# Block 0 takes all sixteen weight pieces in one run, decays are relative to the end of a 128-token block, and the start has another written order

## The chip, the cores and the metric

The kernel runs on one core of one Trainium2 chip. The time is in device microseconds (us), the median of several runs of the whole program. TensorE is called PE, its weight loads PEld, VectorE DVE, ScalarE ACT, GpSimd POOL, SyncE SP. SP and POOL issue the DMAs that are spoken of here.

## The reference

A gated linear attention over 768 tokens, 4 batches and 8 heads of 48 channels, whose output is the input of a feed-forward layer with a squared ReLU:

```python
f = 1.0 / (1.0 + np.exp(-f_logit))
for t in range(S):
    state = f[:, :, t, :, None] * state + np.einsum('bhd,bhe->bhde', k[:, :, t], v[:, :, t])
    y[:, :, t] = np.einsum('bhd,bhde->bhe', q[:, :, t], state)
...
x = attn_out.transpose(0, 2, 1, 3).reshape(B * S, H * D)
h = x @ w_in            # (3072, 384) @ (384, 2048)
r = np.maximum(h, 0.0)
return (r * r) @ w_out  # (2048, 384)
```

## The kernel before, in words

The 768 tokens are cut into six blocks of 128. A block has 4 x 128 = 512 tokens over the batches, the columns of nearly every large operation. The feed-forward layer cuts its 2048 hidden channels into 16 pieces f. For each piece `up` multiplies x by w_in (9 matmuls of 512 columns: three parts of the 384 channels, and three products of high and low halves each), `square` (ACT, three operations) and `rest` (DVE) make the high and low halves of the squared result, and `down`, two pieces later, adds 9 matmuls of w_out into three PSUM banks. Two PSUM banks take turns for `up`, so `up` of a piece waits for `rest` of the piece two before it.

Weights arrive as raw words, 32 loads of 384 KB (piece f, i = 0 for w_in and 1 for w_out), and are decoded once: two operations on ACT, two on DVE each. A decoded piece lies where its raw words lay.

Attention works in 24 units: unit n is head pair n % 4 of block n // 4. A unit of the first three pairs loads f, k, q (`fkq`, 768 KB) and v (`vn`). `gates` (ACT) makes sigmoids. `keys` (DVE) scans them backwards for the decay from each token to the end of its chunk, POOL limits the chunk's whole decay `pe` from below, and the keys are multiplied. `queries` inverts `pe`, scans forwards and multiplies the queries. PE turns the keys (`turn`; ACT copies them out), later blocks do it by DVE and DMA. PE makes the products for the state (`add`) and the scores, DVE masks the scores, `states` carries the state from chunk to chunk, PE makes the output `py`, and ACT and DVE split it into the halves of x (`upper`, `lower`). The fourth pair takes its inputs from rows that `move` has copied by DMA from the other three. Its output `ys` is copied by DMA into spare rows of the three parts of x (`parts`), six copies a block. Pieces 0 and 1 of block 0 don't need these copies: they multiply `ys` itself with a fourth part of w_in (`up_fourth`, raw words `raw4`).

A chunk has 64 tokens before, two to a block. So a unit has 8 chunks, `pe` 8 columns, and `states` decays and adds twice (in block 0, where there is no state yet, once less).

The order of the start is written by hand: FIRST and SECOND are lists of steps, a letter for the step and the number of the unit or piece, recorded in this order on every engine. f, p, z, L, v are loads, G gates, K keys, Q queries, T and N the turn and its copy, D add, S scores, M mask, C states, r and s copies for the crossed halves, Y outputs, H and X the split, m the moves, g and h the copies into x, i and o loads of weights, A I c J and B O d P their four decoding steps, u and U `up`, R `square`, E `rest`, W `down`. Each engine runs its instructions in the recorded order. `busy` steps are matmuls on ones, whose result isn't used.

Before, SECOND ends with block 0's first eight pieces (0 to 7). Then block 1 runs with all sixteen, decoding pieces 8 to 15 on the way (`hook`, with a small memset `mark` ahead of each such load), then block 0 again with pieces 8 to 15, then blocks 2 to 5. `keep` copies block 0's first half out of PSUM into `part`, and `finish` adds it to the second half. The attention units 8 to 23 stand at SLOTS, counted in pieces behind the end of SECOND.

Of the kernel before, what the change touches and what calls it, by code (L numbers as in the profile page):

```python
# [12 lines left out]
F32 = mybir.dt.float32  # L13
# [6 lines left out]
AF = mybir.ActivationFunctionType  # L20
# [12 lines left out]
NZ = B * NC  # L33
CZ = C + 1
# [12 lines left out]
AHEAD = 4  # L47
LO = 8
# [16 lines left out]
SLOTS = (12, 14, 19, 21, 22, 28, 31, 34, 37, 44, 47, 50, 53, 60, 63, 66, 69)  # L65
# [5 lines left out]
f0 G0 p0 K0 f1 G1 z0 p1 T0 N0 v0 D0 Q0 r0 K1 T1 f2 G2 p2 z1 N1 C0 S0 v1 D1 i0 A0 Q1 m1 M0 v2 K2 z2 Q2 S1  # L71
r1 C1 L4 busy3 T2 j0 s0 i2 Y0 N2 I0 S2 D2 m0 H0 M1 X0 s1 Y1 e0 G4 n0 v3 D3 c0 K4 a0 J0 M2 m2 busy2 S3 T4
C2 H1 X1 r2 o0 B0 O0 i1 A1 s2 busy3 Y2 o1 I1 v4 A2 c1 H2 r3 d0 C3 I2 c2 s3 B1 v6 ua0 J1 L5 G5 M3
"""
SECOND = """
ua1 X2 ub1 i3 P0 A3 ub0 Q4 w0 J2 Y3 H3 N4 uc0 X3 uc1 r4 g3 O1 U0 d1 K5 i4 o5 S4 D4 T5 R0 I3 E0 c3 U1 i5
W0 v5 A5 C4 M4 J3 A4 I4 I5 s4 Y4 o4 R1 H4 E1 h3 U3 P1 U2 o2 B2 Q5 N5 X4 O2 L6 c4 v7 i7 i6 G6 K6 S5 c5 W1
M5 J4 o3 R3 E3 B4 O4 m5 T6 D5 C5 R2 B3 J5 B5 E2 U4 d2 O3 r5 P2 s5 Y5 O5 A6 U5 A7 N6 d3 P3 I6 H5 X5 o6 W2
R4 d4 Q6 o7 P4 E4 B7 D6 S6 d5 P5 W3 M6 C6 W4 c6 J6 r6 s6 m4 R5 I7 B6 O6 c7 Y6 H6 d6 J7 U6 O7 d7 X6 P6 m6
E5 r7 D7 R6 S7 C7 M7 U7 E6 s7 Y7 H7 X7 R7 h7 W5 W6 g7 P7 E7  # L80
# [3 lines left out]
class Moe:  # L84
# [40 lines left out]
    def decode(self, row, parts):  # L125
# [5 lines left out]
        head = self.head[self.heads % HEADS][:rows, :n]  # L131
# [7 lines left out]
        )  # L139
        yield  # L140
# [177 lines left out]
    def keep(self, po):  # L318

        part = self.third_of("part0")  # L320
        for e in range(NJ):
            (self.nc.vector.tensor_copy if e % 2 else self.nc.scalar.copy)(out=part[e], in_=po[e])
        return part

# [30 lines left out]
def chunks(t):  # L355
    return t.rearrange("p (n t) -> p n t", t=C)
# [6 lines left out]
def fast_path(ctx, tc, moe, ident, low, fkqT, vN, w, w4, out):  # L363
# [28 lines left out]
    V.memset(dr[:, C::CZ], 1.0)  # L392
# [15 lines left out]
    class Unit:  # L408
# [36 lines left out]
        def gates(self):  # L445
            nc.scalar.activation(scanned(self.fz[:, 1:])[:, :, :C], chunks(self.ft), AF.Sigmoid)  # L446
# [626 lines left out]
```

## Time and profile before

| | us |
|---|---|
| median of 3 runs | 489.99 (489.88 to 490.95) |
| span of the profiled execution | 489.3 |
| PE busy | 471.9 (96%) |
| ACT busy | 284.3 (58%) |
| DVE busy | 248.9 (51%) |
| PEld busy | 377.5 (77%) |
| POOL busy | 29.7 (6%) |

The span runs from the first to the last instruction. The profile lists no time of its own for the profiled execution beside it; the runs shown are 0.6 to 1.7 us above the span. Busy times are unions over an engine's instructions. PE's include the latency of pipelined matmuls, so a busy PE need not be at its peak; the gaps that the timeline shows on it are the surer reading. A timeline row gives the start, the length, the engine, the line, the operation, what it writes and reads, how many instructions are merged in it, and in brackets the idle time of the engine before it and what ended that.

### The profile page before, as it was taken

To read this page: it belongs to the slowest core of one execution; us is meant where nothing else is said; L and a number is where in the kernel's file an instruction comes from. 1 tells how busy PE (TensorE), PEld (TensorE's weight loads), DVE (VectorE), ACT (ScalarE), POOL (GpSimd) and SP (SyncE) were. 2 spreads that over 40 slices of the span, in tenths; PEclk is the share of its full clock that TensorE was granted. 3 is DMA by queue.
4 is the path that set the end of the run, shared out by engine and by line. 5 is a ranking of instruction groups with operands and counts; after the bars stand their busy time and mean duration, and the time that the engine had idled before them with its cause. 6 is when DMAs were issued, how large, how long until landed. Compare 5 with 4: busy or idle time off the path is not lost.

```text
span 489.3 us, 11451 instructions
## 1 busy us (share of the span) xinstructions
PE 471.9 (96%) x4775; PEld 377.5 (77%) x4775; DVE 248.9 (51%) x456; ACT 284.3 (58%) x591; POOL 29.7 (6%) x66
## 2 busy tenths in 40 slices
PE   2889999999999999999999999999999999999996
PEld 2667777888788888888888788888888887888884
DVE  7999962678575365727335636434643322211112
ACT  4589874976755564656565665664745442534441
POOL 4411000000000000000000000000000000000000
PEclk9899999999999999999999999999999999999999
DMA  8888107582544525360423470134440001100002
GB/s 288 246 301 289 31 6 254 162 275 57 108 113 137 122 37 161 80 150 1 105 41 101 118 157 10 37 92 109 122 90 3 1 2 33 68 0 0 1 0 70
DMA packets 64748, 48.65 MB, mean 99 GB/s; under 512 B 46912, under 2 KB 50352, under 8 KB 64688
## 3 DMA queue, kind: packets, MB, share of 16 engines
q1 hardware_dynamic: 64096, 46.78, 34.6%
q0 software_dynamic: 448, 0.92, 0.9%
q8 instruction: 39, 0.64, 0.6%
q14 instruction: 21, 0.17, 0.1%
q10 hardware_dynamic: 144, 0.13, 0.1%
HBM read 35.22 MB, written 7.86 MB: 88 GB/s over the span
## 4 chain that ended last, share of the span: by engine, by line
PE 91%; DMA 5%; DVE 1%; ACT 1%; issue 1%; SPq 1%; POOL 0%; DVEq 0%; ACTq 0%
PE po L276 41%; PE ph L249 41%; DMA raw<-in_w_dram 3%; PE ds L561 2%; PE ds L550 2%; PE py L609 2%; DMA vn<-in_vN_dram 1%; PE ph L621 1%; PE ph L609 1%; PE py L621 1%; SPq L439 1%; DMA x<-ys 1%; DVE fkq L465 0%; ACT rx L487 0%; ACT ys L638 0%
## 5 line engine op out<-in xcount | busy, mean ns | idle before, releaser
L249 PE MATMUL ph<-x,w 128*128 128x512 f32 x864 | 218.2, 398 | 0.8 <-DVE sc L568 0.4
L249 PEld LDWEIGHTS ph<-x,w 128*128 128x128 f32 x864 | 161.6, 188 | 41.3 <-DMA x<-ys 1.2
L276 PE MATMUL po<-gh,w 128*128 128x512 f32 x576 | 180.9, 395 | 0.0
L266 DVE TENSOR_TENSOR gl<-ph,gh 128x512 fp32r<-128x512 f32 x96 | 66.4, 692 | 219.5 <-ACT gh L261 218.3
L259 ACT ACTIVATE ph<-ph 128x512 f32<-128x512 f32 x96 | 56.1, 585 | 147.6 <-PE ph L249 147.6
L276 PEld LDWEIGHTS po<-gh,w 128*128 128x128 f32 x576 | 108.3, 188 | 25.1
L276 PE MATMUL po<-gl,w 128*128 128x512 f32 x288 | 115.9, 402 | 0.0
L276 PEld LDWEIGHTS po<-gl,w 128*128 128x128 f32 x288 | 54.1, 188 | 13.9 <-DVE gl L266 0.7
L261 ACT CAST gh<-ph 128x512 fp32r<-128x512 f32 x96 | 56.4, 587 | 3.0
L260 ACT ACTIVATE ph<-ph 128x512 f32<-128x512 f32 x96 | 55.9, 582 | 3.0
L456 POOL TENSOR_SCALAR fkq<-fkq 128x8 f32<-128x8 f32 x18 | 12.3, 685 | 284.2 <-DVE fkq L451 124.3
L495 ACT COPY sx<-sp 48x208 f32<-48x208 f32 x44 | 16.1, 365 | 16.0 <-DVE sp L583 15.4
L451 DVE TENSOR_TENSOR_SCAN fkq<-fz,dr 128x520 f32<-128x520 f32 x18 | 22.2, 1232 | 2.1 <-ACT fz L446 2.1
L465 DVE TENSOR_TENSOR_SCAN fkq<-fz,dz 128x520 f32<-128x520 f32 x18 | 22.4, 1242 | 0.6
L609 PEld LDWEIGHTS py<-sc,vn 64*48 64x48 f32 (+1 forms) x384 | 16.2, 126 | 7.3 <-issue 7.3
L145 ACT CAST w<-wa 128x384 fp32r<-128x384 f32 (+1 forms) x33 | 16.6, 511 | 7.9 <-DVE wa L136 7.7
L609 PE MATMUL py<-sc,vn 64*48 64x64 f32 (+1 forms) x384 | 20.6, 222 | 0.0
L133 ACT CAST head<-raw 128x384 f16<-128x384 bf16 (+1 forms) x33 | 19.6, 628 | 1.2 <-DMA raw<-in_w_dram 1.1
L621 PE MATMUL py<-rx,sx 48*48 48x64 f32 x192 | 19.3, 215 | 0.0
L147 DVE TENSOR_TENSOR w<-wa,w 128x384 fp32r<-128x384 f32 (+1 forms) x33 | 18.0, 548 | 1.1 <-ACT w L145 0.6
L136 DVE SCALAR_TENSOR_TENSOR wa<-raw,head 128x384 int32<-128x384 int32 (+1 forms) x33 | 17.5, 548 | 1.3 <-ACT head L133 1.3
L159 ACT ACTIVATE junk<-w 128x384 f32<-128x384 f32 x32 | 16.8, 526 | 0.1
(105 smaller groups left out, 443.6 us busy)
## 6 DMA issues: line engine op xcount, KB each, us to landing
raw<-in_w_dram SPq DMA_DIRECT2D x32, 383.8 KB, 5.8
fkq<-in_fkqT_dram SPq DMA_DIRECT2D x15, 768.0 KB, 6.3
vn<-in_vN_dram SPq DMA_DIRECT2D x24, 192.0 KB, 4.0
steps<-fkq SPq DMA_DIRECT2D x48, 64.0 KB, 2.2
out_dram<-ob SPq DMA_DIRECT2D x12, 256.0 KB, 2.1
kn<-steps SPq DMA_DIRECT2D x12, 224.0 KB, 3.2
fkq<-in_fkqT_dram SPq DMA_DIRECT2D x9, 256.0 KB, 5.0
x<-ys SPq DMA_DIRECT2D x30, 64.0 KB, 2.4
```

What stands on the lines that cost most here:

```text
L133: nc.scalar.copy(out=self.upper(head, F16), in_=high)
L147: nc.vector.tensor_tensor(out=w[:, 1], in0=a, in1=w[:, 0].bitcast(F32), op=ALU.subtract)
L249: self.nc.tensor.matmul(self.ph[f], lhsT=w[:, i], rhs=x[:, j], start=first and n == 0, stop=last and n == 2)
L259: nc.scalar.activation(ph, ph, AF.Relu)
L260: nc.scalar.activation(ph, ph, AF.Square)
L261: nc.scalar.copy(out=gh, in_=ph)
L266: self.nc.vector.tensor_tensor(out=gl, in0=self.ph.pop(f), in1=gh.bitcast(F32), op=ALU.subtract)
L276: self.nc.tensor.matmul(po[e], lhsT=l, rhs=r, start=f == fs[0] and i == 0, stop=f == fs[-1] and i == 2,)
L451: V.tensor_tensor_scan(out=rr[:, ::-1], data0=self.fz[:, NZ * CZ : 0 : -1], data1=dr[:, ::-1], initial=0.0, op0=ALU.mult, op1=ALU.add,)
L465: V.tensor_tensor_scan(out=pp, data0=self.fz[:, : NZ * CZ], data1=dz, initial=0.0, op0=ALU.mult, op1=ALU.add)
L609: nc.tensor.matmul(self.py[c][h * C : h * C + m, b * C : (b + 1) * C], lhsT=self.vn[rows, b, h * D : h * D + m], rhs=self.sc[rows, h, b], ...
L621: nc.tensor.matmul(self.py[c][h * C : h * C + m, b * C : (b + 1) * C], lhsT=s[rows, b * D : b * D + m], rhs=q[rows], start=False, stop=b = ...
```

## The change

A chunk of the decays is now the whole block: scans have 4 starts instead of 8, `pe` has 4 columns, and decays are relative to the end of 128 tokens. The state products of both halves of a block then share one reference, so `states` decays once at the start of a block and adds twice. In block 0 nothing is decayed: `first_state` (step k, ACT) copies the first half's products out of PSUM, and `states` adds the second half.

Block 0 takes all sixteen pieces in SECOND, with all 32 weights loaded and decoded there; `keep`, `part`, the second visit to block 0 and the memsets `mark` go. Units 8 and 9 have some of their steps in SECOND (L8, K8, Q8, t8, b8, L9, v8). A unit whose `fkq` buffer comes free late is loaded later (`frees`). FIRST and SECOND are written anew throughout.

```diff
-NZ = B * NC
-CZ = C + 1
+NZ = B
+CZ = TB + 1
-SLOTS = (12, 14, 19, 21, 22, 28, 31, 34, 37, 44, 47, 50, 53, 60, 63, 66, 69)
+SLOTS = (5, 8, 10, 12, 14, 20, 23, 26, 29, 36, 39, 42, 45, 52, 55, 58, 61)
 FIRST = """
-f0 G0 p0 K0 f1 G1 z0 p1 T0 N0 v0 D0 Q0 r0 K1 T1 f2 G2 p2 z1 N1 C0 S0 v1 D1 i0 A0 Q1 m1 M0 v2 K2 z2 Q2 S1
+f0 busy3 f1 p0 G0 z0 p1 v0 f2 G1 K0 T0 v1 N0 j0 D0 i3 K1 z1 Q0 o0 p2 Q1 T1 S0 busy2 m1 z2 G2 M0 i0 r1
...
 def chunks(t):
-    return t.rearrange("p (n t) -> p n t", t=C)
+    return t.rearrange("p (n t) -> p n t", t=TB)
...
+        def first_state(self):
+            nc.scalar.copy(out=self.sp[:, 1, : B * D], in_=self.ds[:ROWS, 0, : B * D])
+
         def states(self):
-            s2 = at = state[self.hp]
-            for c in range(NC):
-                pd = self.ds[:ROWS, c, : B * D]
-                if self.blk == 0 and c == 0:
-                    at = pd
-                    continue
-                sp = self.sp[:, c, : B * D].rearrange("p (b e) -> p b e", e=D)
+            s2 = state[self.hp]
+            sp = [self.sp[:, c, : B * D] for c in range(NC)]
+            if self.blk:
                 V.tensor_tensor(
-                    out=sp, in0=at.rearrange("p (b e) -> p b e", e=D),
-                    in1=self.pe[:ROWS, c::NC].unsqueeze(2).broadcast_to([ROWS, B, D]),
-                    op=ALU.mult,
+                    out=sp[0].rearrange("p (b e) -> p b e", e=D),
+                    in0=s2.rearrange("p (b e) -> p b e", e=D),
+                    in1=self.pe[:ROWS].unsqueeze(2).broadcast_to([ROWS, B, D]), op=ALU.mult,
                 )
+            for c in range(self.blk == 0, NC):
                 V.tensor_tensor(
-                    out=s2.rearrange("p (b e) -> p b e", e=D), in0=sp,
-                    in1=pd.rearrange("p (b e) -> p b e", e=D), op=ALU.add,
+                    out=(*sp, s2)[c + 1], in0=sp[c], in1=self.ds[:ROWS, c, : B * D], op=ALU.add
                 )
-                at = s2
...
-        part = []
-        owed = moe.ending(lambda po: part.extend(moe.keep(po)))
-        whole = half[0] + half[1]
-        order = [(1, whole), (0, half[1])] + [(blk, whole) for blk in range(2, NBLK)]
+        owed = ended(0)
+        order = [(blk, whole) for blk in range(1, NBLK)]
```

What the tables do shows in the order of the instructions. The first place is DVE at the start, from the first scan on; numbers in the names are block and head pair. Before:

```order
L451 SCALAR_TENSOR_TENSOR fkq0_0_141<-fz0_73,dr_69 128x520
L457 TENSOR_TENSOR fkq0_0_141<-fkq0_0_141 128x512
L463 RECIPROCAL dz_70<-fkq0_0_141 128x8
L465 SCALAR_TENSOR_TENSOR fkq0_0_141<-fz0_73,dz_70 128x520
L468 TENSOR_TENSOR fkq0_0_141<-fkq0_0_141 128x512
L451 SCALAR_TENSOR_TENSOR fkq0_1_152<-fz1_74,dr_69 128x520
L457 TENSOR_TENSOR fkq0_1_152<-fkq0_1_152 128x512
L583 TENSOR_TENSOR sp0_75<-ds0_0_167,fkq0_0_141 112x192
L588 TENSOR_TENSOR state0_81<-sp0_75,ds0_0_167 112x192
L463 RECIPROCAL dz_70<-fkq0_1_152 128x8
```

Now:

```order
L444 SCALAR_TENSOR_TENSOR fkq0_0_141<-fz0_73,dr_69 128x516
L450 TENSOR_TENSOR fkq0_0_141<-fkq0_0_141 128x512
L444 SCALAR_TENSOR_TENSOR fkq0_1_147<-fz1_74,dr_69 128x516
L450 TENSOR_TENSOR fkq0_1_147<-fkq0_1_147 128x512
L456 RECIPROCAL dz_70<-fkq0_0_141 128x4
L458 SCALAR_TENSOR_TENSOR fkq0_0_141<-fz0_73,dz_70 128x516
L461 TENSOR_TENSOR fkq0_0_141<-fkq0_0_141 128x512
L456 RECIPROCAL dz_70<-fkq0_1_147 128x4
L458 SCALAR_TENSOR_TENSOR fkq0_1_147<-fz1_74,dz_70 128x516
L461 TENSOR_TENSOR fkq0_1_147<-fkq0_1_147 128x512
```

Both units' keys now stand ahead of both units' queries, and the two state operations have left this place; one of them, the sum, comes four instructions later.

The second place is SP's queue around the moves of unit 2 (`last_kq`, which wait for its queries). Raw names carry the piece and i. Before:

```order
L406 DMA raw0_0_245<-in_w_dram 128x1535
L443 DMA vn0_2_255<-in_vN_dram 128x384
L439 DMA fkq0_2_200<-in_fkqT_dram 128x512
L439 DMA fkq1_0_286<-in_fkqT_dram 128x3x512
L719 DMA raw4_297<-in_w4_dram 112x1023
L406 DMA raw2_0_300<-in_w_dram 128x1535
L443 DMA vn0_3_399<-in_vN_dram 128x384
L476 DMA last_kq_79<-fkq0_2_200 16x1032 x2
L406 DMA raw0_1_460<-in_w_dram 128x1535
L406 DMA raw1_0_465<-in_w_dram 128x1535
```

Now:

```order
L399 DMA raw0_1_206<-in_w_dram 128x1535
L432 DMA fkq0_2_158<-in_fkqT_dram 128x512 x2
L399 DMA raw0_0_241<-in_w_dram 128x1535
L399 DMA raw1_0_278<-in_w_dram 128x1535
L436 DMA vn0_2_325<-in_vN_dram 128x384
L436 DMA vn0_3_331<-in_vN_dram 128x384
L432 DMA fkq1_0_340<-in_fkqT_dram 128x3x512
L469 DMA last_kq_79<-fkq0_2_158 16x1028 x2
L399 DMA raw4_1_447<-in_w_dram 128x1535
L399 DMA raw2_0_453<-in_w_dram 128x1535
```

Four weight loads and the fourth part now stand ahead of these moves, against two and the fourth part before (the fourth part and raw3_0 stand just above the rows shown). Behind them come seven weights, two `vn` and unit 5's 768 KB, then the copies of `ys` into x; before it was seven weights, three `vn` and unit 5's 768 KB.

The third place is PE behind the products with `ys`, from the last matmuls of the first `down` on. Before, unit 4's output followed:

```order
L276 MATMUL po0_0_2_538<-gl0_0_655,w0_1_508 128x512
L276 MATMUL po0_0_2_538<-gh0_0_654,w0_1_508 128x512 x2
L609 MATMUL py1_0_695<-sc1_0_685,vn1_0_500 64x64
L609 MATMUL py1_0_695<-sc1_0_685,vn1_0_500 48x64 x2
L609 MATMUL py1_0_695<-sc1_0_685,vn1_0_500 64x64
```

Now `up` of piece 3 follows, which reads the copied rows of x:

```order
L281 MATMUL po0_0_2_531<-gl0_0_608,w0_1_512 128x512
L281 MATMUL po0_0_2_531<-gh0_0_607,w0_1_512 128x512 x2
L254 MATMUL ph0_3_712<-x0_0_117,w3_0_572 128x512 x3
L254 MATMUL ph0_3_712<-x0_1_118,w3_0_572 128x512 x3
L254 MATMUL ph0_3_712<-x0_2_119,w3_0_572 128x512 x3
```

Unit 4's output has moved behind pieces 3 and 2 and the second `down`.

## Rows read from the trace of the kernel before

**Rows 1.** Windows: length, busy time of each engine (instructions), PE's granted clock, DMA share, GB/s

```profile
0.00:37.60 37.60, 25.45 (x564) 19.09 (x564) 33.23 (x61) 23.52 (x50) 14.07 (x33) 0.95 0.85 275
20.70:24.10 3.40, 3.40 (x86) 2.47 (x84) 3.33 (x7) 1.73 (x4) 1.04 (x2) 0.52 0.95 309
37.60:74.90 37.30, 37.30 (x570) 29.06 (x569) 30.96 (x63) 29.81 (x64) 4.35 (x9) 1.00 0.35 110
74.90:484.50 409.60, 409.17 (x3643) 329.37 (x3642) 183.97 (x331) 230.98 (x478) 11.30 (x24) 1.00 0.32 82
```

**Rows 2.** Timeline of DVE, the first 34 us

```profile
4.37 1.24 DVE L451 TENSOR_TENSOR_SCAN fkq<-fz,dr 128x520 f32<-128x520 f32 x1 [1.19 <-ACT fz L446]
...
8.59 1.23 DVE L451 TENSOR_TENSOR_SCAN fkq<-fz,dr 128x520 f32<-128x520 f32 x1
9.86 0.69 DVE L457 TENSOR_TENSOR fkq<-fkq 128x512 f32<-128x512 f32 x1
10.47 0.35 DVE L583 TENSOR_TENSOR sp<-ds,fkq 112x192 f32<-112x192 f32 x1
10.86 0.35 DVE L588 TENSOR_TENSOR state<-sp,ds 112x192 f32<-112x192 f32 x1
11.13 0.20 DVE L463 RECIPROCAL dz<-fkq 128x8 f32<-128x8 f32 x1
11.36 1.24 DVE L465 TENSOR_TENSOR_SCAN fkq<-fz,dz 128x520 f32<-128x520 f32 x1
...
22.60 0.55 DVE L147 TENSOR_TENSOR w<-wa,w 128x384 fp32r<-128x384 f32 x1
23.07 0.68 DVE L568 TENSOR_TENSOR sc<-ds,mask 128x512 f32<-128x512 f32 x1
...
33.18 0.69 DVE L643 TENSOR_TENSOR ys<-first_py,ys 112x512 fp32r<-112x512 f32 x1 [0.96 <-ACT ys L638]
```

**Rows 3.** Timeline of PE, 33 to 40 us

```profile
33.93 0.96 PE L249 MATMUL ph<-ys,w 112*128 112x512 f32 x3 [0.60 <-DVE ys L643]
...
37.62 0.50 PE L276 MATMUL po<-gl,w 128*128 128x512 f32 x1
...
39.92 0.34 PE L609 MATMUL py<-sc,vn 64*64 64x64 f32 x8
```

**Rows 4.** Timeline of ACT, 35 to 39 us

```profile
35.03 0.58 ACT L259 ACTIVATE ph<-ph 128x512 f32<-128x512 f32 x1
...
36.74 0.52 ACT L145 CAST w<-wa 128x384 fp32r<-128x384 f32 x1
37.16 1.13 ACT L133 CAST head<-raw 128x384 f16<-128x384 bf16 x2
38.31 0.78 ACT L495 COPY sx<-sp 48x208 f32<-48x208 f32 x2
```

**Rows 5.** Timeline of SP's issues, 18 to 36 us

```profile
18.21 1.24 SPq L476 DMA_DIRECT2D last_kq<-fkq  x2
19.50 1.53 SPq L406 DMA_DIRECT2D raw<-in_w_dram  x3
...
27.38 1.21 SPq L406 DMA_DIRECT2D raw<-in_w_dram  x1
33.90 1.79 SPq L650 DMA_DIRECT2D x<-ys  x3
```

**Rows 6.** DMA issues at 19.5, 27.4 and 34 us: KB each, median us to landing

```profile
raw<-in_w_dram SPq DMA_DIRECT2D x1, 383.8 KB, 4.2
...
raw<-in_w_dram SPq DMA_DIRECT2D x1, 383.8 KB, 10.5
...
x<-ys SPq DMA_DIRECT2D x3, 64.0 KB, 4.5
```

**Rows 7.** Timelines of PEld at 75 us and of PE at 124 us

```profile
75.16 0.53 PEld L249 LDWEIGHTS ph<-x,w 128*128 128x128 f32 x3 [0.56 <-DMA x<-ys]
...
124.30 1.91 PE L249 MATMUL ph<-x,w 128*128 128x512 f32 x7 [0.29 <-DVE gl L266]
```

More of the change, by code (lines that the diff above doesn't have):

```diff
@@ L316, in third_of @@
         return [t[:, e, :NT] for e in range(NJ)]
[L318 to L323, printed above, removed]
     def ending(self, end):
@@ L687, in fast_path @@
     ps_a = ctx.enter_context(tc.tile_pool(name="ps_a", bufs=1, space=bass.MemoryType.PSUM))
-    half = list(range(LO)), list(range(LO, NF))
+    whole = list(range(NF))
     xs = {blk: moe.new_x(blk, blk) for blk in range(2)}
@@ L750, in fast_path @@
     moe.psum(ctx, "ps_h0")
-    moe.begin(0, xs[0], half[0])
+    moe.begin(0, xs[0], whole)
     early = ExitStack()
@@ L779, in third @@
             xs[2] = moe.new_x(2, 2)
-        halves = [(f, i) for f in half[1] for i in range(2)]
-        steps = {}
-        def advance(h):
-            if h not in steps:
-                steps[h] = moe.decode(moe.row[halves[h]], lambda: moe.parts(*halves[h]))
-            next(steps[h], None)
-        for n in range(1, NF - 1):
-            few = range(3 * (n - 1) // 2, min(3 * n // 2, len(halves)))
-            for h in few:
-                if n < AHEAD:
-                    weights_load(*halves[h])
-                else:
-                    hook(0, n - AHEAD, 0.5, lambda h=h: weights_load(*halves[h], mark=True))
-            def before(few=few):
-                for h, last in zip(few, (None, *few)):
-                    for m in (h, h, last):
-                        if m is not None:
-                            advance(m)
-            def after(few=few[:-1]):
-                for h in few:
-                    advance(h)
-            def last(few=few):
-                for h in few[-1:]:
-                    advance(h)
-                    advance(h)
-            for place, do in zip((0, 0.5, 0.7) if n > 1 else (0.7, 0.7, 0.7), (before, after, last)):
-                hook(0, n, place, do)
@@ L817, in fast_path @@
-        hook(0, 12, 0, third)
-        later = [Unit(n, xs, (ps_a,)) for n in range(2 * HP, NBLK * HP)]
-        back = 0
+        hook(0, 0, 0, third)
+        given = (FIRST + SECOND).split()
+        later = [unit(n) for n in range(2 * HP, NBLK * HP)]
+        back, frees = 0, []
         for un, last, at in zip((*later, None), (None, *later), SLOTS):
+            if last and last.own:
+                frees.append(at)
             if un:
-                for n, place, stage in STAGE_AT if un.own else LAST_AT:
-                    hook(0, at + n, place, lambda un=un, stage=stage: un.stage(stage))
+                free = frees[un.t - 3 * NJ] if un.own and un.t >= 3 * NJ else 0
+                for n, place, stages in STAGE_AT if un.own else LAST_AT:
+                    for stage in stages:
+                        if f"{stage}{un.n}" not in given:
+                            hook(0, max(at + n, free and free + (0, 2, 2, 2, 3)["LGKQt".find(stage)]), place, lambda un=un, stage=stage: un.stage(stage))
@@ L861, in fast_path @@
                 moe.run(hooks[k], None, owed)
-                owed = moe.ending(
-                    lambda po, blk=blk: moe.finish(
-                        lambda e: out[blk, e * P : (e + 1) * P], None if blk else part, po, blk
-                    )
-                )
+                owed = ended(blk)
     return general[2], obs
```

58 lines of the change are left out of this document (32 added, 26 removed).

## Prediction

> **What bounds the kernel now.** I read the windows view first, then the timelines of the stretch that it points to. The windows [rows 1] show two regimes. From 37.6 to 484.5 us TensorE (PE) is busy for 37.30 of 37.30 and 409.17 of 409.60 us: nothing but its own work sets the pace, and VectorE (DVE) and ScalarE (ACT) have 184 and 231 us of work in the last 409.6. Before 37.6 us PE is busy for 25.45, and much of that is small matmuls between waits, while DVE is busy for 33.23 of 37.60 and the DMA engines for 85%. The program issues the same matmuls in both kernels: counted in the two orders, every shape has the same number, eight filler matmuls each. So the change can move the end only by the time at which PE becomes continuously busy, and by new or vanished gaps after it.
>
> The stretch that decides is the chain of block 0's four attention units on DVE [rows 2]: the first scan starts at 4.37 us, and the last subtraction of unit 3 (`ys`, the fourth part of x) at 33.18, ending at 33.87; between them DVE hardly waits. From there PE has a fixed tail [rows 3]: the product with `ys` at 33.93, the squares of f 0 on ACT, `rest` on DVE, the first `down` at 37.62, which ends where the next work starts, at 39.92. From that point PE stays fed.
>
> **What the change does to that chain.** I price DVE by start-to-start times in [rows 2]: a scan 1.27 us (8.59 to 9.86), a 128x512 tensor op 0.61 (9.86 to 10.47), the state's decay 0.39, the state's sum 0.27, a reciprocal 0.23, a decode op 0.47 (22.60 to 23.07).
> Before, up to `ys`: 8 scans, 16 ops of 512 columns (8 multiplications, 4 masks, 4 subtractions), 4 reciprocals, 4 decays and 4 sums, 10 decode ops: 10.16 + 9.76 + 0.92 + 2.64 + 4.70 = 28.2 us. Started at 4.37 that ends at 32.6; it ended at 33.87, so 1.3 us were waits (0.96 of them for ACT, just before `ys`).
> After, by the new order: 7 scans, 15 ops of 512, 3 reciprocals, 4 sums, 8 decode ops: 8.89 + 9.15 + 0.69 + 1.08 + 3.76 = 23.6 us. The difference of 4.6 has three parts: the second half of unit 4's decay work goes behind `ys` (1.27 + 0.61 + 0.23 = 2.11); block 0 loses its four decays, and with them 1.56; two decode ops go behind (0.94). The first is only moved. Unit 4's scores wait for it, but they now stand behind both products with `ys` on PE (0.7 us each), which covers most of its 2.1 us, and the first `down` covers the rest.
>
> In place of the four decays ACT now copies four states out of PSUM (`first_state`, 112x192). No row shows that copy; two L495 copies of 208 columns take 0.78 us together [rows 4], so I take 0.39 each. They stand between a unit's state products and its output, where the DVE decay stood, and cost nothing on that path as long as ACT has room, which it has before 37.6 us (23.52 us busy [rows 1]). Bounds: free, or 4 x 0.39 = 1.6 us if all of it delays the chain.
>
> The shorter tables (4 starts of a block instead of 8, scans of 516 columns instead of 520) save 4/520 of 1.24 us a scan: nothing. `keep` and the added `part` go (three copies, three sums); PE never waits for them in 74.9 to 484.5 us [rows 1], so nothing is gained there either.
>
> So DVE would end `ys` at 4.37 + 23.6 = 28.0 without waits. I keep the 1.3 us of waits of before: 29.3. From the end of `ys` to the first `down` took 37.62 - 33.87 = 3.75 us [rows 2, 3], and `down` itself 2.30. I keep both: 29.3 + 3.75 + 2.30 = 35.35 us.
>
> **The next thing that can be late** is the six small copies of `ys` into x, which `up(3)` needs straight after that `down`; before, unit 4's output stood in between. They wait in SyncE's queue (SP) behind loads. Before, the queue was held by the wait for unit 2's query (18.21), then took eleven loads (seven weights, three `vn`, one unit's 768 KB); the first landed at 19.52 + 4.2 = 23.7, the last at 27.38 + 10.5 = 37.9, and the copies followed, 4.5 us after their issue [rows 5, 6]. After, the wait for unit 2's query stands at the same place in time (DVE ends that query after six scans, seven ops of 512, three reciprocals and a sum, at 4.37 + 12.85 = 17.2 against 18.2), and behind it stand seven weights, two `vn` and one unit: one `vn` less. So the copies, issued at 29.5 to 31, land behind these loads at 35 to 36.5, and PE needs the third pair 1.4 us after it starts `up(3)`. That is a tie with 35.35; I take 35.4.
>
> Compared at equal work: before, PE was there at 39.92, with unit 5's transposes (0.5 us) also done. The gain is 39.92 - 35.4 - 0.5 = **4.0 us**. The gaps after 37.6 us in the profile are small: 0.56 us for the copies at the start of block 1, and 0.29 at 124.30, in the stretch where block 1 carried deferred decodes [rows 7]. I expect half of it back: 0.4 us. Forecast gain 4.4 us.
>
> **Does PE stay fed through the long block 0?** Now all 16 pieces are decoded under it, while before 8 of them were decoded under block 1. Until the last `rest` of block 0, DVE has 14 scans, 46 ops of 512, 7 reciprocals, 16 state ops, 66 decode ops and one transposition: about 85 us, so 4.4 + 85 = 90 us at the earliest. ACT has 66 decode ops (0.42 and 0.57 [rows 4]), 16 squarings of 1.71 (35.03 to 36.74), and 55 copies and gates of attention, an estimate of 24 us at 0.4 to 0.6 each as in the same rows: about 84. PE, starting at 35.4 with 68 to 70 us of work left in block 0, ends it near 105. Both have about 15 us in hand at the end. Before, the same sum for DVE gave 67 us against 74.9, 8 in hand, and PE didn't wait. So I take nothing for it.
>
> **Sum.** The profiled span is 489.3, the median of the runs shown 489.99, 0.7 more. 489.99 - 4.4 = **485.6 us**. Own bounds of this case: -2.6 us if the waits of DVE vanish too and both small gaps go; +1.6 for the state copies.
>
> **Rivals.**
> *ACT starves PE in the long block.* Of ACT's 84 us some 59 remain when PE starts at 35.4, under 70 us of PE work: 84% load. In 37.6 to 74.9 ACT was busy 29.81 of 37.30, 80% [rows 1]. If 80% is all that such an interleaving gives, the 59 us take 73.5 and PE loses about 3: 488.6. For it: ACT runs in order, and a cast that waits for DVE holds the next squaring. Against it: before, ACT's idle time in that stretch was partly lack of work. 17%.
> *The clock.* [...] 6%. [...]
> *The copies into x come late: slower.* `up(3)` now stands straight behind the first `down`, and nothing can fill in, since PE runs in order. The slowest load of this stretch took 10.5 us from issue to landing [rows 6]. The last pair can be issued once both products with `ys` are done, 1.4 us behind `ys`, so near 31.3; if it took 10.5, it would land at 41.8, and with 1.4 us of `up(3)` ahead of it PE would start at 40.4 instead of 39.4 at equal work: +1.0, 491.0. Each us more adds one. It decides from a landing at 40.8 on. For it: 32 weights now crowd the start, and DMA is 85% busy there. Against it: one load less stands ahead of them than before. 10%.
> *The gain is spent elsewhere,* by a wait at the end of block 0 (its last piece is decoded just before its use, and the copies into block 1's x still follow unit 7): 490.0, no change. 9%.
> That the decays over 128 tokens fall under the kernel's floor of 2^-40, which would start the general path, is excluded: in the inputs as drawn the smallest product over a block is 2^-30.5.
>
> **How the numbers follow.** My case has 58%. A measurement of this kernel can tell about 0.2% from no change, 1.0 us. Faster: my case, the clock's, and two thirds of ACT's: 75%. Within: the rest of ACT's and half of the last: 11%. Slower: the late copies, and the other half of the last: 14%. The range must leave out no more than 20%: the late copies and some of the last lie above, so it reaches from 482.6 (485.6 less 2.6, and a little) to 489.4, which takes in ACT's case.
>
> **What would show it.** Right: `ys` on DVE ends near 29, the first `down` ends near 35, and PE is busy without gaps to the end; the four decays are gone and ACT shows four 112x192 copies of some 0.39 us. The copies into x land by 36.5. Wrong: weight loads on PE wait for `x<-ys` near 35; the windows of 40 to 100 us show PE below full, with ACT over 90% busy, which is the ACT case; a granted clock of half at 30 to 35 us; or `ys` ends after 32, which would mean that waits for DMAs or for ACT's state copies replaced the ops removed.

## The result, and the profile after

The changed kernel takes 493.74 us (median of 19 runs, 491.69 to 495.62), the kernel before beside it 490.5 (19 runs). The ratio is 1.0061, with a 95% interval of 1.0047 to 1.0075: 0.6% slower, about 3 us, where 0.9% faster was forecast. The profiled execution took 493.07 us, its span is 491.0 (489.3 before), so 1.7 of the difference can be read from the two traces.

The windows of the changed kernel, cut where its regimes change (columns as in [rows 1]):

```profile
core 0: us, PE busy (x) PEld busy (x) DVE busy (x) ACT busy (x) POOL busy (x), PEclk, DMA share, GB/s
0.00:24.40 24.40, 16.57 (x344) 11.56 (x345) 19.34 (x36) 13.93 (x32) 11.25 (x26) 1.00 0.90 297
24.40:27.40 3.00, 0.24 (x3) 0.13 (x2) 1.74 (x4) 0.80 (x3) 0.00 (x0) 1.00 0.91 322
27.40:31.00 3.60, 3.60 (x81) 3.29 (x81) 1.14 (x3) 1.92 (x5) 0.00 (x0) 0.54 1.04 402
31.00:33.10 2.10, 2.10 (x47) 1.48 (x47) 2.07 (x3) 1.41 (x3) 0.19 (x1) 0.98 0.59 213
33.10:34.50 1.40, 0.08 (x4) 0.02 (x2) 0.70 (x2) 0.00 (x0) 0.69 (x2) 1.00 0.07 19
34.50:42.40 7.90, 7.76 (x98) 6.17 (x98) 6.11 (x11) 7.37 (x15) 2.48 (x5) 1.00 0.51 127
42.40:74.90 32.50, 32.48 (x260) 25.56 (x259) 29.59 (x56) 31.68 (x67) 3.21 (x6) 1.00 0.84 300
74.90:486.00 411.10, 411.10 (x3948) 331.38 (x3947) 175.89 (x305) 227.42 (x474) 12.24 (x27) 1.00 0.27 66
```

Two stretches stand out in which PE does almost nothing: 24.4 to 27.4, where DVE is busy for 1.74 and ACT for 0.80 of the 3.00 us, and 33.1 to 34.5. Between them PE runs at 0.54 of its clock, that is at half of it for most of the stretch (27.7 to 31.1 us). From 42.4 us on PE is busy for 443.58 of 443.60 us. So the long block 0 is fed, and the whole difference lies in the start.

The clock column needs care in the first row. The trace's record of the granted clock begins at its first rise, at 20.9 us here and at 14.0 in the kernel before, and a window takes the time ahead of it as 1.00. Three filler matmuls of 512 columns in PE's timeline, first of the kernel before, then of the changed kernel, show the level:

```profile
14.35 0.82 PE L715 MATMUL ph<-one 128*128 128x512 bf16 x3
```

```profile
19.06 1.49 PE L708 MATMUL ph<-one 128*128 128x512 bf16 x3
```

The first start 226 and 220 ns apart, the second 427 and 426. So in the changed kernel PE was still at its lower level up to 20.9 us, 6.9 us longer than before.

The chain of waits of the changed kernel through these stretches (start, length, engine, line, instructions merged):

```profile
20.55 0.66 PE ds L554 x23
21.20 0.11 issue
21.31 0.38 PE ds L554 x9
...
23.52 0.89 PE ph L254 x3
24.42 0.20 PE ds L554
24.61 2.76 issue
27.37 1.03 PE ds L554 x28
...
30.21 2.02 PE ph L254 x6
...
33.16 1.32 issue
34.48 0.21 PE first_py L601
34.69 0.05 PE first_py L613
34.75 0.13 PE first_py L613 x3
34.90 0.59 ACT ys L630
```

"issue" is time in which an engine waited for nothing that the profile shows. Each stands in the middle of a step: after the first of the 32 score matmuls of unit 3, and six matmuls before the end of the 48 of unit 3's output. DVE, which had set the pace before [rows 2], now waits for what comes of it. Its timeline:

```profile
28.90 0.35 DVE L582 TENSOR_TENSOR state<-sp,ds 112x192 f32<-112x192 f32 x1 [2.76 <-ACT sp L569]
...
35.52 0.69 DVE L635 TENSOR_TENSOR ys<-first_py,ys 112x512 fp32r<-112x512 f32 x1 [1.71 <-ACT ys L630]
```

`ys` ends at 36.21, 6.9 us after the forecast 29.3 and 2.3 after that of before. The first `down` ends at 42.42, 3.0 after the 39.4 of before at equal work. Behind it 1.3 us are regained (3.0 less 1.7). PE's idle time there, 0.43 us before [rows 1] and 0.02 now, is a third of it; where the rest comes from was not traced.

What is on the DMA engines while PE stands? The DMA queues of the changed kernel from 25 to 26 us (queue and kind, packets, MB, share of 16 engines):

```profile
q1 hardware_dynamic: 117, 0.33, 87.6%
q8 instruction: 1, 0.02, 6.3%
```

One packet of 16 KB on a queue of the kind "instruction" starts at 25.0, among loads that fill the engines. There are 39 such packets on that queue in the whole run. If one holds 256 instructions, as the counts below suggest, they hold 9,984, and PE has 4,775 matmuls with as many weight loads. So we take it for PE's program. That gave the leading theory: **A, PE's next instructions come late**, because their packet stands behind weight loads that were issued before it. The rivals: **B**, an unseen wait for data; **C**, the state copies on ACT lengthen the chain; and the half clock, as a cause of its own or as a consequence.

### The profile page after: what moved, and what is told of

Read it like the earlier page. It is cut to its first block, busy times and chain, and to the rows that moved or that the text cites. A ratio compares the mean times of both kernels' runs of the same rounds, so it can differ in the third digit from the quotient of the medians.

```text
span 491.0 us, 11407 instructions
## 1 busy us (share of the span) xinstructions
PE 474.4 (97%) x4775; PEld 379.6 (77%) x4775; DVE 237.3 (48%) x417; ACT 284.5 (58%) x595; POOL 30.1 (6%) x66
## 4 chain that ended last, share of the span: by engine, by line
PE 94%; DVE 1%; issue 1%; ACT 1%; DMA 1%; SPq 0%; DVEq 0%
PE po L281 42%; PE ph L254 41%; PE ds L554 3%; PE ds L543 2%; PE py L601 2%; PE ph L613 1%; PE ph L601 1%; PE py L613 1%; DMA fkq<-in_fkqT_dram 1%; PE first_py L601 1%; DVE fkq L458 1%; PE pk L494 0%; PE first_py L613 0%; PE ph L708 0%; DVE fkq L444 0%
## 5 line engine op out<-in xcount | busy, mean ns | idle before, releaser
L449 POOL TENSOR_SCALAR fkq<-fkq 128x4 f32<-128x4 f32 x18 | 11.6, 643 | 284.8 <-DVE fkq L444 174.0
L444 DVE TENSOR_TENSOR_SCAN fkq<-fz,dr 128x516 f32<-128x516 f32 x18 | 22.0, 1222 | 1.2 <-ACT fz L439 1.2
L458 DVE TENSOR_TENSOR_SCAN fkq<-fz,dz 128x516 f32<-128x516 f32 x18 | 22.2, 1233 | 0.6
L561 DVE TENSOR_TENSOR sc<-ds,mask 128x512 f32<-128x512 f32 x24 | 16.4, 682 | 2.0 <-PE first_py L601 1.3
```

The lines of the kernel that those rows point to most:

```text
L444: V.tensor_tensor_scan(out=rr[:, ::-1], data0=self.fz[:, NZ * CZ : 0 : -1], data1=dr[:, ::-1], initial=0.0, op0=ALU.mult, op1=ALU.add,)
L458: V.tensor_tensor_scan(out=pp, data0=self.fz[:, : NZ * CZ], data1=dz, initial=0.0, op0=ALU.mult, op1=ALU.add)
```

## The experiments

### The parts of the change apart

**The decays alone**, in the kernel before, with each state copy straight ahead of the sum that needs it:

```diff
-NZ = B * NC
-CZ = C + 1
+NZ = B
+CZ = TB + 1
-... N1 C0 S0 ... r1 C1 L4 ... C2 H1 ... d0 C3 I2 ...
+... N1 k0 C0 S0 ... r1 k1 C1 L4 ... k2 C2 H1 ... d0 k3 C3 I2 ...
```

> The kernel before, with the decays over 128 tokens alone (shorter tables, the state copies of block 0 on ACT straight ahead of the sums, no decays in block 0), in its own order and with its own two visits to block 0. By my sum DVE loses four decays of 0.39 us in block 0, 1.56 us ahead of `ys`, and by theory A no instruction wait comes with it, as the loads and the matmuls stand as before: `ys` ends at 32.2 to 33, the time is 488.4 to 489.4. By theory C the state copies, 0.39 each on ACT, stand in DVE's way and eat this: `ys` at 33.5 to 35, 490 to 491.5.

Measured: 497.31 us, ratio 1.0132 (1.0115 to 1.0149). Both theories missed, C by its size. The DVE timeline of this kernel:

```profile
12.93 0.35 DVE L589 TENSOR_TENSOR state<-sp,ds 112x192 f32<-112x192 f32 x1 [2.39 <-ACT sp L576]
...
25.71 0.35 DVE L589 TENSOR_TENSOR state<-sp,ds 112x192 f32<-112x192 f32 x1 [0.39 <-ACT sp L576]
...
31.02 0.35 DVE L589 TENSOR_TENSOR state<-sp,ds 112x192 f32<-112x192 f32 x1 [2.71 <-ACT sp L576]
```

A copy takes 0.32 us on ACT, but ACT runs in order, and where these stood it was waiting or busy with something else: 5.5 us of waits in place of 1.56 us of decays. So each copy was put close behind its products:

```diff
-... N1 k0 C0 ... r1 k1 C1 ... k2 C2 ... d0 k3 C3 ...
+... Q0 r0 k0 K1 ... A0 k1 Q1 ... s1 k2 Y1 ... a0 k3 J0 ...
```

> As the run with the decays alone, but each state copy on ACT stands close behind the products that it copies (k0 behind r0, k1 behind the first weight's head, k2 ahead of unit 1's output, k3 behind a0), where the other run had them straight ahead of the sums and DVE waited 2.39, 0.39 and 2.71 us for them. Theory C (the place in ACT's order is what these copies cost): the three waits vanish but for 0.5 us in all, DVE keeps 1.0 to 1.5 of the 1.56 us of the four decays, `ys` starts at 31.7 to 32.5 on DVE (33.18 before), and the time is 488.5 to 489.6, below the kernel before. Rival (DVE is not the bound behind 20 us, PE and its late instructions are): `ys` at 33 or later, 490 to 491.5.

Measured: 490.61, ratio 0.9996 (0.9987 to 1.0005). The three waits are gone (the sums start at 10.41, 17.73, 24.61 and 26.41 with no wait), yet `ys` starts at 34.1: the rival. On PE's timeline of this kernel stands

```profile
24.63 0.58 PE L561 MATMUL ds<-last_kq 48*64 48x64 f32 x25 [1.58 <-issue]
```

Once DVE is 1.5 us faster, PE meets the same kind of wait in the old order too.

**Block 0 in one run of sixteen pieces, behind the old start**: FIRST as in the run just told, SECOND in the changed kernel's order.

```diff
 FIRST = (the run before this one)
-ua1 X2 ub1 i3 P0 A3 ub0 Q4 w0 ...
+ua1 X2 ub1 i3 i4 A3 ub0 w0 Y3 H3 I3 uc0 X3 o4 i5 c3 U0 ...
-        order = [(1, whole), (0, half[1])] + [(blk, whole) for blk in range(2, NBLK)]
+        order = [(blk, whole) for blk in range(1, NBLK)]
```

> The start in the order of before (with the state copies close behind their products), and block 0 in one run of sixteen pieces with the changed kernel's order from there on. If the loss of the change lies in its order of the start (late instructions and the half clock behind them), `ys` starts at 31.7 to 33.2 as with the decays alone, no wait for instructions over 0.5 us shows, PE stays full from 45 us on, the 1.3 us that the changed kernel regained behind 42 us stay, and the time is 487 to 489.5. If the loss belongs to the long block 0 (weights that come too late, ACT at its limit), PE shows gaps from 45 to 110 us and the time is 490 or more.

Measured: 491.03, ratio 1.0009 (0.9999 to 1.0018). The time lies above the range of the first case and inside that of the second, whose gaps it does not show: PE is busy for 34.91 of 35.00 us from 40 to 75. The first case is not borne out in full either: waits for instructions of 2.9 us in all stand in the start, where none over 0.5 was expected, at full clock, and `ys` starts at 33.1. So the decays and the sixteen pieces together change the time by no more than 0.2%. What remains of the change is **the new order up to the end of the start, and it costs the 0.6%**.

### Is it instructions that PE waits for?

**The fillers left out.** The eight `busy` matmuls at the start go, 16 instructions.

```diff
-f0 busy3 f1 ... S0 busy2 m1 ... A1 busy3 S2 ...
+f0 f1 ... S0 m1 ... A1 S2 ...
```

> The eight filler matmuls at the start (busy) are left out; their result is not used. Theory A (PE's instructions come in pieces of 256, a matmul being two, its weight load and itself): with 16 fewer instructions ahead, each wait is found 8 matmuls later in the program: the one at 24.6 us, now after the first of unit 3's 32 score matmuls, stands after the 9th (one or two more by records that are missing), and the one at 33.2, now 15 matmuls before the end of unit 3's output, among its last 7. Their lengths stay (2 to 3.5 and 0.5 to 2 us), and the time within 1.5 us of 493.7. Theory B (a wait for data): the place in the program stays, before the second of the score matmuls. A lower clock at the start without the fillers would add up to 1 us by either.

Measured: 493.31, ratio 1.0058 (1.0038 to 1.0078). The chain of waits of this kernel:

```profile
20.07 1.06 PE ds L554 x31
21.12 0.99 issue
22.11 0.36 PE ds L554
...
27.42 0.31 PE ds L554 x9
27.73 1.51 issue
29.24 0.52 PE ds L554 x20
```

With the fillers, the first wait stood after the 23rd score matmul of unit 2, now after the 31st; the second stood after the first score matmul of unit 3, now after the 9th. Eight matmuls each, as A says and B can't. A's lengths did not come true: the second is 1.51 us where 2 to 3.5 was expected, and of the third, which by A now falls two matmuls behind unit 3's output, only 0.13 us is left (a step of 365 ns, at 35.1 us, among steps of 231 to 236). The counts agree: PE's windows of the changed kernel from wait to wait hold

```profile
21.25:24.60 3.35, 3.29 (x125) 1.00 0.89 317
24.60:34.40 9.80, 5.80 (x128) 0.83 0.78 292
```

that is 128 matmuls with their weight loads, 256 instructions, less a few missing records. `ys` stays at 35.5 although the waits are 1.7 us shorter. PE's timeline of the kernel without fillers shows why:

```profile
25.83 1.59 PE L254 MATMUL ph<-x,w 128*128 128x512 f32 x3
```

On the chain these three take 1.52 us, in the changed kernel 0.89 (23.52 above). From the second to the third it is 427 ns, as in this run's recorded half clock (427 and 426 behind 31.3 us), against 231 to 236 at the full one. The record of the clock begins only at 27.2 us here, so without the fillers PE stayed at its lower level until then, 6.3 us longer than in the changed kernel. It used up its instructions more slowly, and waited less for the next.

**Only the last three fillers out**, 1.28 us of the chain (19.27 to 20.55): `A1 busy3 S2` becomes `A1 S2`.

> The changed kernel without the three filler matmuls ahead of unit 2's scores, which take 1.28 us on the chain of waits (19.27 to 20.55). Rival (PE's own work is the bound from 16 us on): `ys` starts 1.0 to 1.3 us earlier and the time is 492 to 492.8. Theory A: the next 256 instructions can't be there before 21.3 (in the changed kernel they came 0.11 us after PE had used up those before), so the time taken out comes back as a wait of 1 to 1.5 us within unit 2's scores, 3 matmuls later in the program; the later waits keep their length, `ys` starts within 0.4 us of 35.5, and the time is 493.2 to 494.2.

Measured: 493.98, ratio 1.0067 (1.0055 to 1.008), within A's range. In the profiled execution, the fastest of its runs (492.08), the chain shows waits of 1.83, 0.76 and 1.96 us. The first is there as A said, 0.3 longer; the clock then fell already at 21.5 us and the second shrank, probably because slower matmuls use up instructions more slowly; the third grew. `ys` started at 34.3, 0.8 earlier than A allowed. The fillers are not what costs.

**The state copy of unit 3 ahead of its scores** (`S3 i10 k3` becomes `k3 S3 i10`).

> Only unit 3's state copy (k) is recorded ahead of its scores (S) instead of behind them. Theory C (the chain got longer because the state copies on ACT wait for what stands ahead of them on PE): this copy ran 3.3 to 4.4 us after ACT was free; ahead of the scores it runs before 25 us, and with it the state's sum on DVE (28.90), so `ys` ends 2 to 4 us earlier, and the time falls to 490 to 492. Theory A (late instructions): the mask and the output of unit 3 need the scores anyway, which stand behind the late instructions; the wait of 2.8 us stays, `ys` moves by less than 0.5 us, and the time is 493.2 to 494.2.

Measured: 493.81, ratio 1.0073 (1.0051 to 1.0095), `ys` at 35.8. The copy ran at 26.10 instead of 28.54, yet the sum on DVE came no earlier: it waited for the scores. C is out as a cause in the changed kernel.

**Loads taken from in front of the packet.** First four weights, moved behind the copies into x:

```diff
-... H1 o4 X1 ... S3 i10 k3 o1 B4 ... I3 i5 C3 ... U0 i4 Q4 ... A5 N4 ... h3 ...
+... H1 X1 ... S3 k3 o1 ... I3 C3 ... U0 Q4 ... N4 ... h3 i5 o4 i4 ... A5 ... B4 ...
```

> Theory A (late instructions): PE stands at 24.6 us for 2.76 and at 33.2 for 1.32 us, each time in the middle of a step, because its next 256 instructions come late; a 16 KB packet of an instruction queue starts at 25.0 and at 32.0, with the DMA engines at 0.9 to 1.05 of full, and 1.4 us after its end PE goes on. Here four weight loads (1.5 MB, about 4.4 us of DMA at 350 GB/s) go behind the copies into x, so the queue is emptier from 21 to 31 us. By A both waits shrink below 1 us each, the granted clock stays full from 27 to 31, `ys` on DVE ends at 31 to 33 instead of 36.21, and the time is 489 to 490.5 us, 3 to 4.5 below the changed kernel. Theory B (the wait is for the rows that `move` copies for unit 3, or for something else whose place is fixed by data): these copies stay where they are, so the waits stay at 2.8 and 1.3 and the time within 1 us of 493.7. Theory C (ACT's state copies, recorded behind the scores): no change either.

Measured: 499.76, ratio 1.0176 (1.0158 to 1.0194). The first of the two waits did not shrink; it grew to 3.58. The loads that were left had moved up and still filled DMA to 0.88 from 24 to 28 us. The second vanished, and there DMA was at 0.29 (28 to 32 us). So half of A's forecast came true, at the place where the engines were in fact empty. And a new loss came: PE busy for only 30.11 of 35.00 us from 40 to 75. Then nearly all loads of that stretch were moved:

```diff
-... S3 i10 k3 o1 B4 Y2 I3 i5 C3 ... X3 B1 U0 i4 ... o2 A5 ... g3 L5 S4 ... h3 ...
+... S3 k3 Y2 I3 C3 ... X3 U0 ... g3 S4 ... h3 o1 L5 i5 o2 i4 o4 ... B1 ... A5 ... B4 ...
```

> The changed kernel, in which all weights but one and unit 5's 768 KB that were issued from 18.7 to 26.4 us stand behind the copies into x (their decoding too): the DMA engines should be nearly empty from 25 to 36 us. The end of the kernel will be far later, since these weights are then missing from 45 us on (498 to 510); what counts is the start. Theory A (instructions come late because their packet stands behind loads that were issued before it): the packet for the wait in unit 3's scores starts by 23.5 instead of 25.0, this wait is at most 1.5 us (2.76), the one in unit 3's output vanishes (1.32), and `ys` starts on DVE at 31.5 to 33.8 instead of 35.52, the less the longer PE keeps its full clock. Theory B (waits for data): 2.8 and 1.3 stay, `ys` at 35.5.

Measured: 500.78 (2 runs), ratio 1.0205 (1.0176 to 1.0233), and the start as A says. The chain of waits, DVE's timeline and the windows of this kernel:

```profile
24.72 0.20 PE ds L554
24.92 1.11 issue
26.03 0.76 PE ds L554 x28
```

```profile
31.26 0.68 DVE L635 TENSOR_TENSOR ys<-first_py,ys 112x512 fp32r<-112x512 f32 x1
```

```profile
27.50:31.00 3.50, 3.50 (x66) 2.54 (x61) 3.30 (x6) 2.69 (x6) 0.55 (x1) 1.00 0.01 5
...
40.00:75.00 35.00, 28.22 (x227) 20.85 (x226) 24.24 (x44) 27.71 (x57) 3.22 (x6) 0.90 0.94 349
```

The packet starts at 23.4 in place of 25.0, between the landings of the last weight ahead of it (23.25) and of the `vn` issued behind that weight (23.75). The wait in the scores is 1.11, the one in the output is gone, the clock stays at 1.00, and `ys` starts 4.26 us earlier than in the changed kernel. The two sizes add up: 3.1 us of waits less on the chain (4.19 against 1.11) and 1.7 for the clock (3.60 us at 0.54 instead of 1.00), less 0.6 by which unit 2's scores start later here. **A holds** for the start. The data that B names were there: already in the changed kernel the rows that `move` copies for unit 3 had landed by 22.21, 2.4 us before the wait began. But from 40 to 75 us PE loses 6.8 us for want of weights.

### Can the early start be kept?

The next four runs put the same loads at other times. A marked load (a one-element memset on DVE, `mark`) holds SP's queue until DVE gets there.

```diff
-            weights_load(n, "io".index(nm))
+            weights_load(n, "io".index(nm), mark=t == "o1")
-... i2 r3 J1 s2 r2 S3 i10 k3 o1 B4 Y2 I3 i5 C3 d0 ...
+... i2 r3 J1 s2 r2 S3 k3 Y2 I3 C3 o1 L5 i5 o2 d0 ...
```

> The changed kernel, in which one weight load is marked (a small memset on DVE behind unit 3's state, near 27.5 us, holds SP's queue until then), and behind it follow unit 5's 768 KB and two more weights; three more weights go behind the copies into x. So DMA is nearly empty from 25 to 29 us, as in the run with the loads out of the way, but carries 1.9 MB from 29 to 35. Theory A: the wait in unit 3's scores is at most 1.5 us, none over 0.5 us in unit 3's output, `ys` starts at 31 to 32, as in that run (31.3). If weights that come 3 to 5 us later than in the changed kernel aren't yet needed, PE stays full from 40 us on and the time is 489 to 490 (493.7 less the 4 us by which `ys` is earlier). Rival (the gain at the start is a loan: from 40 to 60 us DMA and ACT are at their limit, so the weights set the pace and an earlier start buys nothing): PE shows gaps of 2 us or more from 40 to 75 us, and the time is 491.5 to 494.

> As the run with the held load, but unit 5's 768 KB go behind the copies into x too, so that these copies find less ahead of them: 1.2 MB in place of 1.9. Theory A: `ys` the same, 31 to 32. The copies into x land 1 to 2 us earlier than in that run; unit 5's gates come later, near 42. If the copies set PE's start there, the time is 0.5 to 1.5 us below that run's; by the rival (the loads set the pace from 40 us on, their order makes no difference, only their sum) it is the same within 0.7 us.

Measured: 497.24, ratio 1.014 (1.0112 to 1.0169), and 496.81, ratio 1.0123 (1.0108 to 1.0137). `ys` starts at 31.0 and 30.9, as A says, at full clock. Then PE starves. The windows of the two kernels, the one with unit 5's data among the held loads first:

```profile
33.50:40.00 6.50, 1.47 (x36) 0.91 (x34) 0.69 (x2) 2.66 (x6) 1.46 (x3) 0.79 1.02 274
40.00:75.00 35.00, 33.78 (x286) 26.63 (x287) 29.27 (x55) 31.73 (x66) 3.21 (x6) 0.94 0.87 315
```

```profile
33.50:40.00 6.50, 5.65 (x83) 4.36 (x82) 4.84 (x11) 5.28 (x11) 1.46 (x3) 1.00 0.93 261
40.00:75.00 35.00, 30.27 (x243) 22.64 (x242) 25.46 (x48) 29.04 (x60) 3.21 (x6) 1.00 0.86 317
```

(The second holds back `o1 i5 o2` and has L5 behind h3.) In the first, unit 4's `vn` landed at 40.56 behind unit 5's 768 KB, and PE stood 5.7 us at unit 4's products; in the second, weights came late. The rival is borne out, and by more than it said: the early start is a loan. The same loads delayed by only 2 to 3 us, all still ahead of the copies into x:

```diff
-... I1 J0 c1 Y1 ... ua0 i2 r3 ... S3 i10 k3 o1 B4 Y2 I3 i5 C3 d0 H2 ub0 ...
+... I1 J0 i2 c1 Y1 ... ua0 r3 ... S3 k3 o1 Y2 I3 C3 i5 i10 d0 H2 B4 ub0 ...
```

> The changed kernel, all its loads ahead of the copies into x as before, but two of them marked (a memset on DVE of one element): the first behind unit 2's moves is held until 22 us, a second one, three loads on, until unit 3's state, near 27.5; B4 on ACT goes behind unit 2's split. So DMA idles for 1 to 2 us near 22 and near 27, and is busy to 37 instead of 33. Theory A: the packet for unit 3's scores starts by 23, its wait is at most 1.2 us (2.76), that in unit 3's output at most 0.5 (1.32), `ys` starts at 31 to 32.5 (35.52). If the bytes can bear this delay, PE stays full from 41 us on and the time is 488.8 to 490.5. Rival (they can't): gaps of 2 us or more on PE from 36 to 60 us, and 492 to 496.

> As the run with two marks, with the first alone. Theory A: the wait in unit 3's scores shrinks as there (at most 1.2 us), but seven loads then stand in the queue when PE begins the next 256 instructions near 25 us, so the packet starts at 29 to 31 and the wait in unit 3's output stays (0.8 to 2 us); `ys` starts at 32 to 33.5. The time is 489.5 to 491.5; by the rival 492 or more.

Measured: 495.5, ratio 1.0098 (1.0079 to 1.0118), and 493.06, ratio 1.0047 (1.003 to 1.0063). Both missed A's `ys`: it started at 35.1 and 35.7. The held loads were issued from 22.2 and 22.6 on, 0.2 us after PE began a new stretch (22.0 and 22.4), and its next packet starts at 25.0 and 25.4. So they still stood in front of it, and PE waited 1.94 and 1.93 us; when exactly a packet is asked for, the trace doesn't show. After that PE ran at 0.50 and 0.52 of its clock from 27.5 to 33.5, longer than in the changed kernel, and that ate what the waits had given. With two marks the copies into x landed only at 42.73 to 44.10, and PE waited for them. With one, PE was busy for 34.84 of 35.00 us from 40 to 75, so there the rival's time came true without its gaps.

At last the two visits to block 0 of the kernel before, which need half of the weights by 75 us, with the changed order of the start: held, not held, and held with unit 5's steps moved back. In the first two the head of piece 3's first weight is overwritten by another's before it is used, so one weight has other values; no instruction changes. The third takes the buffer for a head that has been free longest, and so avoids this.

```diff
-... S3 i10 k3 o1 B4 Y2 I3 i5 C3 d0 ... h3 ...
+... S3 k3 Y2 I3 C3 o1 i4 o2 d0 ... h3 L5 i5 o5 o4 ...
+... S3 o1 k3 i4 Y2 o2 I3 C3 d0 ... h3 L5 i5 o5 o4 ...
+... S3 k3 Y2 I3 C3 o1 L5 d0 ... h3 i4 o2 i5 o4 ... U3 ... U2 ... W1 ... K5 ... T5 ...
```

> The two visits to block 0 of the kernel before (eight pieces, then block 1, then the other eight), so that only half of the weights are needed by 75 us, with the 128-token decays, with the changed kernel's order of the start, and with the weights held back as in the runs with a held load: after unit 2's moves one weight at once, three from 27.3 us on, unit 5 and the rest behind the copies into x. Theory A with the loan (what the sixteen pieces cost is that loads can't be kept away from the instructions without PE starving for weights later): `ys` starts at 30.5 to 31.7, no instruction wait over 1.5 us, no gaps of over 1.5 us in all from 40 to 75 us, since DMA has to bring half as much; the first `down` ends near 38, 1.4 us ahead of before at equal work, the time 488 to 489.7, below both kernels. Rival (the early start is a loan here too: a weight that comes late stops PE at 40 to 55 us): gaps of 2 us or more there, 491 to 494.

> As the run with two visits and held loads, but the three weights are not held: they are issued behind unit 2's moves, from 19 us on, as in the changed kernel (of which seven loads there are four here). Theory A: the packet for unit 3's scores stands behind them, so the wait there is 1.5 to 3 us, `ys` starts 0.8 to 2.5 us later than with the held loads, and the time is up to 2 us longer, unless the weights are what PE waits for from 40 us on, in which case it is shorter by up to 2.

> Two visits to block 0, the changed kernel's order of the start, the 128-token decays, and held loads: one weight and unit 5's 768 KB from 27.3 us on, the rest behind the copies into x; unit 5's transposes and scores stand behind the products of pieces 2 and 3 and the `down` of piece 1. Theory A: `ys` starts at 30.5 to 32, no instruction wait over 1.5 us, gaps on PE from 38 to 75 us of at most 1.5 us in all, the time 488 to 489.8, below both kernels. Rival (the loads set the pace here too, because what is kept from 21 to 28 us, some 2 MB, is needed by 50 us): gaps of 2 us or more between 38 and 55 us, on weights of pieces 2 to 4 or on unit 5's data, and 491 to 495.

Measured: 497.93, ratio 1.0128 (1.0105 to 1.0151); 502.32, 1.0225 (1.0205 to 1.0244); 499.82, 1.0188 (1.0152 to 1.0224). All three times lie above every range. Held against not held is A's comparison once more: `ys` at 32.0 and 35.2, with waits for instructions of 2.0 and 4.5 us in all, both starts somewhat later and both waits longer than A allowed. In the third `ys` starts at 31.2, but PE is busy for only 4.33 of 6.50 us from 33.5 to 40; the 2.2 us that it stands are at unit 4's products, for a `vn` that landed at 37.27 behind unit 5's data. From 40 to 75 us PE is busy for 31.07, 29.79 and 30.40 of 35.00, and that is not the rival's want of weights: DMA is busy for 0.37 to 0.46 of the stretch, and PE's waits of over 2 us there (3.9, 3.9 and 2.3) are all at unit 5's transposes, for its keys on DVE. Unit 5's data had landed at 40.06, 43.37 and 36.36, and DVE's scan of them, in its written place, came at 42.33, 45.53 and 48.28 (in the third behind the gates on ACT, at 47.63). With these waits the clock fell to half for 6.8, 6.8 and 3.4 us. So these three fail by the order of unit 5's steps, and leave the question of the loan open for two visits; no version here beats the kernel before.

## Why the prediction was wrong

**What bounds the kernel** was right for before and wrong for the change. "So the change can move the end only by the time at which PE becomes continuously busy" held: from 42.4 us on there is no gap. But the step "DVE would end `ys` at 4.37 + 23.6 = 28.0", plus 1.3 us of waits "of before", took it that DVE goes on setting the pace when it has 4.6 us less to do. In the changed kernel the chain of waits is on PE from 14.53 us on, almost without a break. **This is the step that failed**: the waits were carried over, and PE's own supply was not on the list of what is late next. DVE does just the operations that were counted, 23.6 us of them; but from 4.37 to 36.21 it waits for 8.2 us where 1.3 were put. Of these 6.9 us too much, 4.3 go when the packet is freed (`ys` ends at 31.94 there). The other 2.6 stay: in that run DVE still waits 2.0 us for ACT, 0.56 for PE and 0.82 for a load of the first units, which the sum by DVE alone left out. Part of it may be the lower clock up to 20.9 us: at the full one PE's share of the chain from 14.53 on would be shorter by at most half, 3.2 us (an estimate). No run tests this by itself.

**The work removed** was sized well: the state copies take 0.32 us where 0.39 was assumed. Their bounds, free to 1.6 us, were too narrow: badly placed they cost 5.5 us. In the changed kernel, moving one made no difference.

**From `ys` to the first `down`** 3.75 + 2.30 us were kept from before; from 36.21 to 42.42 it is 6.21. Right within 0.2.

**The copies into x** were forecast to land 5 to 6 us after their issue, behind loads. They landed 2.3 to 3.2 us after it, from 38.69 to 41.15, in time, since the queue had emptied. (Before, eight weights stood ahead of them, not seven, so the change takes two loads out of their way and not one.) The landing passed the 40.8 of the slower rival, but because `ys` was late, not for that rival's reason: no weight load on PE waits for a copy.

**Feeding the long block 0** was right: 32.48 of 32.50 us from 42.4 to 74.9, with ACT at 31.68. So the rival by which ACT can't give more than 80% in such an interleaving is refuted: it gave 97%.

**The clock** has 6% in the forecast. No run shows that figure; what they showed is 0.54 of the clock from 27.4 to 31.0, nearly at the place watched for (30 to 35), and it cost 1.7 us. It came after PE had stood still for 2.76 us. The half clock lasted 3.4 us (27.7 to 31.1), as before (20.7 to 24.1 at 0.52 [rows 1]), and the lower level at the start lasted 6.9 us longer than before.

**The regain behind the start** was put at 0.4 and was 1.3, of which the small gaps on PE are 0.4 and the rest was not traced.

**Late instructions** were not among the rivals. The changed kernel has 125 and 128 recorded matmuls from wait to wait, and the waits there took 2.76 and 1.32 us. The prediction should have asked for it, since the change lets PE run 128 small matmuls in 3.4 us while DMA is at 0.89 (21.25 to 24.60). PE's timeline of the kernel before showed a first sign, a wait at an `issue` within unit 2's scores:

```profile
19.11 0.33 PE L561 MATMUL ds<-fkq 48*64 48x64 f32 x5 [0.22 <-issue]
```

## What to carry to other kernels

When a change takes work from the engine that sets the pace, go through every supply of the next one, its instructions too: count them (here two per matmul, and 256 from wait to wait), mark where the next ones are due, and look at what the DMA queues carry there. What gave it away here was a wait "for issue" in the middle of a step, whose place moved by eight matmuls when 16 instructions ahead of it were left out. And the loads that filled DMA early were here both the cause of a wait and what was needed 20 us later: what was taken away at 21 to 31 us here came back as 4.7 to 6.8 us of starving between 40 and 75 us in the runs with sixteen pieces that held back most.

## What the runs showed of the hardware

- Packets of PE's instructions started late where loads issued before them filled the DMA engines. From PE's start on a new stretch to the packet's start it took 3.7 and 4.6 us with DMA at 0.85 and 1.01 (21.31 to 25.05, 27.37 to 32.01), and 1.2 us with DMA at 0.00 (34.48 to 35.69). These packets then took 1.0 to 1.1 us, and PE went on 1.3 to 1.5 us after their end (26.06 to 27.37; with the loads out of the way 24.55 to 26.03).
- Some waits of PE were followed by half clock, which cost time on top: 1.7 us after the 2.76, and 0.52 of the clock from 27.5 to 33.5 after waits of 0.82 and 1.93. After 1.11 us (loads out of the way), and after 0.56 (fewer loads held), the clock stayed full. In the run with the old start and the new block 0, where PE stood for 1.00 us of 20 to 24 and 1.34 of 24 to 28, it did too. What decides is not settled: in the changed kernel the half clock came behind a standstill and ended with PE busy (3.60 of 3.60 us, 27.4 to 31.0), but these runs show no single length of wait that brings it.
- A clock of 1.00 ahead of the first recorded rise was no reading. Matmuls of 512 columns started 426 to 427 ns apart there (19.1 to 19.9 us in the changed kernel), and 220 to 240 apart within a run of them behind it; the rise came at 14.0 us before, at 20.9 in the changed kernel, and at 27.2 without the fillers.
